# Retention by chunks and a two-layer PReLU block in one program: second batch in parts, last block through all units at once

## The chip, the cores and the metric

The kernel runs on one core of a Trainium2 chip. The metric is the device time of one execution in microseconds (us); lower is better. A profile of one execution shows what each engine did: PE is TensorE's matmuls and PEld its weight loads, DVE is VectorE, ACT is ScalarE, POOL is GpSimd, SP is the engine whose queue issues nearly all DMAs.

## What is computed

For 8 batches and 8 heads, with 576 positions and 64 features a head, retention is a causal product without softmax; its output, heads side by side, is the input of a two-layer block with a PReLU between.

```
scores = scale * q @ k.T                       # per batch and head, 576 x 576
ret    = scores * gamma[h] ** (i - j) for i >= j, else 0
attn   = ret @ v                               # 8 x 8 x 576 x 64, float32
x      = attn.transpose(0, 2, 1, 3).reshape(4608, 512)
h      = x @ w_in                              # 512 -> 2048
g      = max(h, 0) + alpha * min(h, 0)
out    = g @ w_out                             # 2048 -> 512
```

## The kernel before

**Tiles.** The 4608 rows of x are 18 blocks of 256 (`kb`). The 2048 hidden columns are 8 units of 256 (`u`). A cell is one unit of one block: a first product (`unit`, L1079, 24 matmuls of 128 x 256 columns) into the PSUM banks psh, an ACT and DVE chain that makes g (L1087 to L1094), a split of g for the next product (`split_g`, two ACT and two POOL operations, L1103 to L1110), and a second product (`second`, L1128, 12 matmuls of 128 x 512) into the four banks pso, two cells later (LAG). Precision: x, w and g are split into three pieces each, and each product is three matmuls of pieces. The first eight cells (blocks 0 and 1, units 0 to 3) are computed with plain float32 matmuls instead (`unit_plain` L1014, `second_plain` L1045).

**Weights.** There are 32 pieces of weight (4 a unit). They come as 8-byte words and are converted (`convert`: two ACT, three DVE and one POOL operation, L657 to L681), the first 16 in the start and the other 16 during the pass over the blocks, in the tile wa, from where they are stored (`w32`). `split_w` makes three pieces of a weight (ACT L705, POOL L706, DVE L709). SBUF holds the pieces of four units. So the program goes through all blocks with units 0 to 3, keeping partial sums in DRAM (`o_kept`) and x too (`x_kept`), and then through them with units 4 to 7. At the turn, blocks 14 to 17 are visited in a zigzag of two units a visit, in thirteen visits, so that one weight of a new unit can be split while another is in use. Each visit splits x (`split_x`, L980 to L997) and ends with an evacuation of pso (L1146 to L1151).

**Attention.** Positions are in 9 chunks of 64. Batch 0 is computed in three parts of 4, 4 and 1 chunks for all heads at once (`load_part`, `part_transposes` L447, `part_scale` POOL L421, `part_scores` L473, `part_states` L495, `part_carry`, `part_values` L536 and L552, `last_part` L580 to L613), so that the first block of x is there early. Batches 1 to 7 are computed in pairs of heads (32 pairs, numbers 4 to 31 here; `joint`): the ninth chunk's scores (L838, into a psh bank), scores of eight chunks (L846) and their states (L855), both in the two psa banks, chunks of even and odd number in different banks; DVE masks them (L898, L905) and adds the states up (L916 to L927); the values (L787) of a pair are computed in the next pair's joint. The pairs of batch 1, FIRST, use ACT and POOL for some of it (L873, L883, L889, L934) in place of DMA and DVE.

**Order.** Operations are recorded by `do` with an engine, a cost and what they read and write. `plan` then orders them: from due times and the costs in `do` it picks, engine by engine, what runs next, and knows of banks, of the DMA backlog, and of the SBUF port that DVE and POOL share (operations with `lock=True`). Each engine executes its list in that order. Where a room is used again, its next user waits for the last one.

Of the kernel before, what the change touches and what calls it, by code (L numbers as in the profile page):

```python
# [21 lines left out]
def kernel(  # L22
# [316 lines left out]
    LAG, FIRST, APART = 2, range(4, 8), range(5, 8)  # L339
    QUEUE, HOLD_X = (), 100.0  # L340
    GROUPS = (("v0",), ("v1",), ("x",), ("s", "u"))
# [17 lines left out]
    gs = [slot(mlp, f"g{n}", [P, 3, 2, TB]) for n in range(2)]  # L359
    gas = [slot(mlp, f"ga{n}", [P, 2, TB]) for n in range(2)]  # L360
    gts = [slot(mlp, f"gt{n}", [P, 2, TB]) for n in range(2)]
# [16 lines left out]
    room = {(s, i): Gen(wsl[s, i]) for s in range(1, NS) for i in range(4)}  # L378

    def spot(s, i, at, n):  # L380
        return lambda: room[s, i].get().rearrange("p a b -> p (a b)")[:, at * TB:(at + n) * TB]

    def spot_p(x, i):
        return spot(x + 1, i, 0, 4) if x < 2 else spot(3, 0, 2 * i, 2)

    def key_p(x, i, m):
        return (room[x + 1, i], "d", m) if x < 2 else (room[3, 0], "d", i)

    def part(x, i):
        return spot_p(x, i)().rearrange("p (m h d) -> p m h d", h=H, d=D)  # L390

    def sums_of(x, j):
        return spot(x + 1, j // 2, 4 + j % 2, 1)().rearrange("p (c d) -> p c d", d=D)

    def sums_key(x, j):
        return room[x + 1, j // 2], "u", j

    def carry_of(x):
        return spot(1 + x, 1 + x, 4, 1)().rearrange("p (c d) -> p c d", d=D)

    def carry_key(x):
        return room[1 + x, 1 + x], "c"

    def load_part(x, which=(0, 1, 2)):
        j0, j1 = PARTS[x]
        for i in which:
            for m in range((j1 - j0 + 1) // 2):
                s0 = (j0 + 2 * m) * C
                rows = min(P, j1 * C - s0)
                dma(lambda i=i, m=m, rows=rows: part(x, i)[0:rows, m],  # L410
                    lambda i=i, s0=s0, rows=rows: (k, q, v)[i][0, :, s0:s0 + rows].rearrange(
                        "h p d -> p h d"), rows * DM * 4, (), [key_p(x, i, m)],
                    "ACT" if x == 0 and i == 1 else "SP", RATE_256)

    def part_scale(x, i):
        j0, j1 = PARTS[x]
        rows = min(P, (j1 - j0) * C)
        for m in range((j1 - j0 + 1) // 2):
            def f(m=m):
                t = part(x, i)[0:rows, m]  # L420
                nc.gpsimd.tensor_tensor(  # L421
                    out=t, in0=t, in1=tp[0:rows, i - 1, m, :, None].to_broadcast([rows, H, D]),
                    op=ALU.mult)
# [4 lines left out]
    def banks_of(x):  # L428
        while True:
            for b in (psa[0], pso[0], pso[1], pso[2], pso[3]) if x == 0 else (psa[0], psh[1]):  # L430
                yield b

    def part_transposes(x, i, bank):
        t = tT[x, i] = Gen(gs[0]) if x == 0 and i else room[1, 3] if x == 0 else \
            room[2 + i, 3 - 2 * i]

        def at():
            return (t.get().rearrange("p a b c -> p (a b c)") if x == 0 and i else
                    t.get().rearrange("p a b -> p (a b)"))[:, 0:1024].rearrange(
                        "p (c s) -> p c s", c=NPAIR)  # L440
# [16 lines left out]
    def part_scores(x, bank):  # L457
        a = Gen(gs[1]) if x == 0 else room[3, 2]

        def at():  # L460
            return (a.get().rearrange("p a b c -> p (a b c)") if x == 0 else
                    a.get().rearrange("p a b -> p (a b)"))[:, 0:1024].rearrange(
                        "p (h n) -> p h n", h=2)
# [21 lines left out]
    def part_states(x, bank):  # L485
# [16 lines left out]
        for j in range(4):  # L502
            was = sums_key(x, j - 1) if j else carry_key(x) if x else None

            def g(j=j):
                if j == 0 and x == 0:
# [14 lines left out]

    def part_values(x, bank):
        a, at = tat[x]
        qt, qT = tT[x, 1]
        gx = xb[x] = Gen(xs[x])
# [16 lines left out]
        for m in range(2):  # L542
            js = [j for j in (2 * m, 2 * m + 1) if j or x]
# [15 lines left out]
        def xt():  # L559
            return gx.get().rearrange("p c (m q s) -> p q c m s", m=2, q=2)  # L560
        do("ACT", 0.59, lambda: nc.scalar.copy(xt()[:, 0], to(0)), [(pv[0], 0)], [(gx, "p", 0)])
        for h2 in range(2):
            do("ACT", 0.59, lambda h2=h2: nc.scalar.copy(xt()[half(h2), 1], to(1)[half(1 - h2)]),
               [(pv[1], 0)], [(gx, "p", 1 + h2)])

    def last_part():
        t = room[3, 3]

        def tt():
            return spot(3, 3, 0, 2)().rearrange("p (i c s) -> p i c s", i=2, c=NPAIR)  # L570

        def at():
            return spot(3, 3, 2, 2)().rearrange("p (h c s) -> p h c s", h=2, c=NPAIR)
        pt = Gen(psa[0])

        def f():
            to = pt.get().rearrange("p (i c s) -> p i c s", i=2, c=NPAIR)
            for i in range(2):
                for c in range(NPAIR):
                    nc.tensor.transpose(to[:, i, c], part(2, i)[0:C, 0, 2 * c:2 * c + 2].rearrange(  # L580
                        "p h d -> p (h d)"), ident[0:C, 0:C])
        do("PE", 0.8, f, [key_p(2, 0, 0), key_p(2, 1, 0)], [(pt, 0)])
# [19 lines left out]
        def f():  # L602
            to = pv.get()[:, 0:NPAIR * C].rearrange("p (c s) -> p c s", c=NPAIR)
            for c in range(NPAIR):
                for h2 in range(2):
                    nc.tensor.matmul(to[half(h2), c], part(2, 2)[0:C, 0, 2 * c + h2],
                                     at()[0:C, h2, c], start=(c == 0), stop=False,
                                     skip_group_check=True)
            for c in range(NPAIR):
                for h2 in range(2):  # L610
                    for e in range(0, D, 32):
                        o = h2 * D + e
                        nc.tensor.matmul(to[o:o + 32, c], carry_of(2)[half(h2), c, e:e + 32],  # L613
                                         tt()[half(h2), 1, c], start=False, stop=True,
                                         skip_group_check=True)
        do("PE", 0.9, f, [key_p(2, 2, 0), (t, "m", 0), (t, "m", 1), (t, "t"), carry_key(2)], [(pv, 0)])
        gx = xb[2] = Gen(xs[2])
        do("ACT", 0.37, lambda: nc.scalar.copy(
            gx.get()[:, :, 0:C], pv.get()[:, 0:NPAIR * C].rearrange("p (c s) -> p c s", c=NPAIR)),
            [(pv, 0)], [(xb[2], "b", 0)])  # L620
# [74 lines left out]
    def split_w(at, room_=None):  # L695
        u, i = divmod(at, 4)
        if room_:
            g = Gen(room_)
            key = (g, "w", 0)
            dma(lambda: words_of(g)[:, 0:DM], lambda: w32[at], P * DM * 4, [(w32m[at], 0)], [key])  # L700
        else:
            key = plain[at]
        w = w_at[u, i] = Gen(wsl[u % NS, i])
        full = lambda: words_of(key[0])[:, key[2]:key[2] + DM]
        do("ACT", 0.64, lambda: nc.scalar.mul(piece(w.get()[:, 0]), full(), BELOW), [key], [(w, 0)])  # L705
        do("POOL", 1.29, lambda: nc.gpsimd.tensor_tensor(  # L706
            out=piece(w.get()[:, 1]), in0=full(), in1=w.get()[:, 0], op=ALU.subtract),
            [key, (w, 0)], [(w, 1)], lock=True)
        do("DVE", 0.70, lambda: nc.vector.scalar_tensor_tensor(  # L709
            out=piece(w.get()[:, 2]), in0=w.get()[:, 0], scalar=ONE, in1=full(), op0=ALU.mult,  # L710
            op1=ALU.subtract), [key, (w, 0)], [(w, 2)], lock=True)
# [5 lines left out]

    def load_kq(n):
        b, c = pairs[n]
        if n in APART:  # L720
            kx = qx = Gen(wsl[n - 4, 0])
            kx.kx = lambda: words_of(kx)[:, 0:S]
            qx.qx = lambda: words_of(qx)[:, S:2 * S]
        else:
            kx, qx = Gen(kxs), Gen(qxs)
            kx.kx, qx.qx = kx.get, qx.get
        loaded[n] = [kx, qx, None, vnm[n % 2]]
        for x, g, src in (("qx", qx, q), ("kx", kx, k)):
            for a in range(4):
                f0 = (a % 2) * 32  # L730
                dma(lambda t=getattr(g, x), a=a: t().rearrange("p (n r) -> p n r", r=32)[
                        32 * a:32 * a + 32],
                    lambda src=src, a=a, f0=f0: src[b, 2 * c + a // 2].rearrange(
                        "(n t) d -> t n d", t=32)[:, :, f0:f0 + 32], S * P, (), [(g, x, a)],
                    "ACT" if n in QUEUE and x == "qx" else "SP", RATE_128)

    def load_kn(n):
        b, c = pairs[n]
        kn = loaded[n][2] = Gen(kns[n % 2])
        for h2 in range(2):  # L740
            dma(lambda h2=h2: kn.get()[half(1 - h2)],
                lambda h2=h2: k[b, 2 * c + h2].rearrange("(j t) d -> t j d", t=C), S * D * 4, (),
                [(kn, h2)], "ACT" if n in QUEUE else "SP", RATE_256)
# [8 lines left out]
    def operands(n):  # L752
# [3 lines left out]
        def f():  # L756
            qh = qx.qx().rearrange("p (j x r) -> p j x r", x=2, r=32)
            nc.gpsimd.tensor_tensor(out=qh, in0=qh,
                                    in1=tabx[:, None, c, :, None].to_broadcast([P, NJ, 2, 32]),
                                    op=ALU.mult)  # L760
        four = [(qx, "qx", a) for a in range(4)]
        do("POOL", 1.15, f, (), four, lock=True)
        kT, qT = turned[n] = Gen(kTs[n % 2]), Gen(qTs[n % 2])
        for to, x, g in ((kT, "kx", kx), (qT, "qx", qx)):
            do("DVE", 0.77, lambda to=to, fro=getattr(g, x): nc.vector.transpose(to.get(), fro()),
               [(g, x, a) for a in range(4)], [(to, 0)])
# [9 lines left out]
    def values(n, pv):  # L776
# [6 lines left out]
        for i, js in enumerate((range(0, j1), range(j1, NJ))):  # L783
            def f(i=i, js=js):
                for j in js:
                    for h2 in range(2):
                        nc.tensor.matmul(pv[i].get()[half(h2), (j - js[0]) * C:(j - js[0] + 1) * C],  # L787
                                         vns[n % 2][:, h2, j], mt.mt()[:, h2, j], start=True,
                                         stop=True)
            parts.append((0.133 * len(js), f, [(vn, x, h2) for x in "vs" for h2 in range(2)] +  # L790
                          [(mt, x, h2) for h2 in range(2) for x in ("q", 0, 1, "x")],
# [20 lines left out]

    def on_pe(parts, groups):
        for some in groups:
            do("PE", sum(parts[x][0] for x in some), lambda some=some: [parts[x][1]() for x in some],
               [key for x in some for key in parts[x][2]],
               [key for x in some for key in parts[x][3]], kind="half" if not {"v0", "v1"} & set(some) else None)

    def joint(n):
# [11 lines left out]
        ps = [Gen(psa[p2]) for p2 in range(2)]  # L831

        def at(p2):
            return ps[p2].get().rearrange("p (i j s) -> p i j s", i=2, s=C)

        def f():
            for h2 in range(2):
                nc.tensor.matmul(pv[1].get()[half(1 - h2), 7 * C:], kT.get()[half(h2), chunk(NJ - 1)],  # L838
                                 qT.get()[half(h2), chunk(NJ - 1)], start=True, stop=True)
        parts["x"] = 0.03, f, [(kT, 0), (qT, 0)], [(pv[1], "x")]  # L840

        def f():
            for j in range(NJ - 1):
                for h2 in range(2):
                    x = half((1 - h2, h2)[j % 2])
                    nc.tensor.matmul(at(j % 2)[x, 0, j // 2], kT.get()[half(h2), chunk(j)],  # L846
                                     qT.get()[half(h2), chunk(j)], start=True, stop=True,
                                     skip_group_check=True)
        parts["s"] = 0.47, f, [(kT, 0), (qT, 0)], [(ps[0], 0), (ps[1], 0)]

        def f():
            for j in range(NJ - 1):
                for h2 in range(2):
                    x = half((h2, 1 - h2)[j % 2])
                    nc.tensor.matmul(at(j % 2)[x, 1, j // 2], kn.get()[half(1 - h2), j],  # L855
# [483 lines left out]
```

## Time and profile before

| | us |
|---|---|
| median of 3 runs | 961.99 (961.79 to 962.37) |
| the profiled execution | 960.84 |
| its span, first to last instruction | 959.1 |
| from the start to the first split product | 107.3 |

| stretch of the span, us | PE busy | DVE | ACT | POOL |
|---|---|---|---|---|
| 0 to 107.3 | 91.7 | 86.5 | 71.6 | 71.2 |
| 120 to 440 | 318.0 | 236.4 | 203.4 | 213.7 |
| 440 to 545 | 100.1 | 76.5 | 77.4 | 83.6 |

The groups that matter, one row each, with the mean of one operation in ns: L1079 first product 284 (24 to a cell, overlapping), L1128 second product 393 (12 to a cell), L898 masks 483 (96), L916 sums 492 (56), L709 split weight on DVE 964 to 1300, L706 on POOL 1272 to 1498, L669 on the tile wa 924, L705 split weight on ACT 626 to 630.

How to read it: matmuls overlap, so PE's mean duration is not PE's price; the price is the time from the start of one group to the start of the next. A chain piece called "issue" is time in which the engine waited for nothing that the profile shows. DMA share is the mean busy share of the core's 16 DMA engines.

### The profile page before, as it was taken

To read this page: it belongs to the slowest core of one execution; us is meant where nothing else is said; L and a number is where in the kernel's file an instruction comes from. 1 tells how busy PE (TensorE), PEld (TensorE's weight loads), DVE (VectorE), ACT (ScalarE), POOL (GpSimd) and SP (SyncE) were. 2 spreads that over 40 slices of the span, in tenths; PEclk is the share of its full clock that TensorE was granted. 3 is DMA by queue.
4 is the path that set the end of the run, shared out by engine and by line. 5 is a ranking of instruction groups with operands and counts; after the bars stand their busy time and mean duration, and the time that the engine had idled before them with its cause. 6 is when DMAs were issued, how large, how long until landed. Compare 5 with 4: busy or idle time off the path is not lost.

```text
span 959.1 us, 22745 instructions
## 1 busy us (share of the span) xinstructions
PE 927.6 (97%) x8713; PEld 815.9 (85%) x8713; DVE 623.4 (65%) x1292; ACT 592.7 (62%) x1329; POOL 633.0 (66%) x515
## 2 busy tenths in 40 slices
PE   5998799999999999999899999999999999999997
PEld 4766598889888888888788899999999999999996
DVE  6789877777767778777678767564444544444444
ACT  3669756666657576665877666655555555555542
POOL 4759876658758577494887989665555555555543
PEclk9999999999999999999999999999999999999999
DMA  9977687777767778776464644242222112122111
GB/s 235 200 167 149 167 176 189 161 189 187 172 161 175 190 168 182 187 169 177 175 220 143 194 137 132 88 121 78 89 88 67 67 66 67 66 67 66 45 45 66
DMA packets 253341, 131.66 MB, mean 137 GB/s; under 512 B 218144, under 2 KB 218160, under 8 KB 253232
## 3 DMA queue, kind: packets, MB, share of 16 engines
q1 hardware_dynamic: 251120, 129.67, 52.2%
q8 instruction: 68, 1.11, 0.5%
q10 hardware_dynamic: 2112, 0.53, 0.3%
q14 instruction: 41, 0.34, 0.1%
HBM read 81.67 MB, written 35.13 MB: 122 GB/s over the span
## 4 chain that ended last, share of the span: by engine, by line
PE 82%; DVE 3%; ACT 1%; issue 1%; POOLq 0%; POOL 0%; DVEq 0%; ACTq 0%
PE psh L1079 39%; PE pso L1128 37%; PE psh L787 3%; PE psa L846 1%; PE psa L855 1%; DVE wa L667 1%; PE psh L838 1%; DVE ga L1094 0%; DVE o L1151 0%; DVE wa L669 0%; DVE ga L1088 0%; DVE at L898 0%; DVE lx L987 0%; ACT lx L980 0%; ACT psh L1091 0%
## 5 line engine op out<-in xcount | busy, mean ns | idle before, releaser
L1079 PEld LDWEIGHTS psh<-lx,w 128*128 128x128 f32 x3264 | 410.3, 191 | 21.0 <-DVE ga L1094 5.7
L1079 PE MATMUL psh<-lx,w 128*128 128x256 f32 x3264 | 418.8, 284 | 6.1 <-DVE ga L1094 3.3
L1128 PE MATMUL pso<-w,g 128*128 128x512 f32 x1632 | 403.5, 393 | 1.0 <-DVE o L1151 0.7
L1128 PEld LDWEIGHTS pso<-w,g 128*128 128x128 f32 x1632 | 295.8, 189 | 58.0 <-DVE o L1151 1.1
L1107 POOL TENSOR_TENSOR g<-ga,g 128x512 fp32r<-128x512 f32 x136 | 178.0, 1309 | 235.2 <-ACT g L1103 230.5
L1088 DVE SCALAR_TENSOR_TENSOR ga<-psh,gt 128x256 f32<-128x256 f32 x272 | 114.6, 422 | 173.9 <-ACT gt L1087 165.1
L1110 POOL TENSOR_TENSOR g<-g 128x512 fp32r<-128x512 f32 x136 | 177.1, 1302 | 10.8 <-ACT g L1105 0.7
L1094 DVE SCALAR_TENSOR_TENSOR ga<-psh,malpha,ga 128x256 f32<-128x256 f32 x272 | 130.0, 479 | 65.2 <-ACT psh L1091 63.8
L1091 ACT ACTIVATE psh<-ga 128x256 f32<-128x256 f32 x272 | 105.2, 388 | 97.3 <-DVE ga L1088 96.2
L1103 ACT ACTIVATE g<-ga 128x512 fp32r<-128x512 f32 x136 | 86.0, 632 | 117.8 <-PE pso L1128 106.0
L1087 ACT COPY gt<-psh 128x256 f32<-128x256 f32 x272 | 101.1, 372 | 70.8 <-PE psh L1079 62.4
L997 POOL TENSOR_TENSOR lx<-lx 128x512 fp32r<-128x512 f32 x78 | 100.6, 1298 | 17.7 <-DVE lx L987 15.6
L1105 ACT ACTIVATE g<-ga 128x512 fp32r<-128x512 f32 x136 | 84.4, 620 | 0.0
L898 DVE SCALAR_TENSOR_TENSOR at<-psa,pf,mask 64x256 f32<-64x256 f32 x96 | 46.3, 483 | 19.9 <-PE psh L787 10.1
L980 ACT ACTIVATE lx<-x 128x512 fp32r<-128x512 f32 x78 | 48.5, 628 | 0.0
L994 POOL TENSOR_TENSOR lx<-x,lx 128x512 fp32r<-128x512 f32 x30 | 38.8, 1293 | 7.4 <-ACT lx L992 7.3
L1146 DVE TENSOR_TENSOR op<-pso,op 128x512 f32<-128x512 f32 x46 | 31.5, 684 | 14.1 <-PE pso L1128 14.1
L787 PEld LDWEIGHTS psh<-at,vn 128*64 128x64 f32 x900 | 29.0, 138 | 9.6 <-issue 3.6
L987 DVE TENSOR_TENSOR lx<-x,psa 128x512 fp32r<-128x512 f32 x48 | 32.6, 678 | 4.4 <-PE psh L1079 4.3
L787 PE MATMUL psh<-at,vn 128*64 128x64 f32 x900 | 33.6, 226 | 1.5 <-DVE ga L1094 1.5
L806 ACT COPY x<-psh 128x256 f32<-128x256 f32 (+3 forms) x84 | 24.2, 319 | 17.1 <-PE psh L787 11.3
L1151 DVE SCALAR_TENSOR_TENSOR o<-pso,op 128x512 f32<-128x512 f32 x46 | 31.6, 688 | 1.1
(183 smaller groups left out, 864.6 us busy)
## 6 DMA issues: line engine op xcount, KB each, us to landing
ok<-o SPq DMA_DIRECT2D x46, 256.0 KB, 2.9
x<-xk SPq DMA_DIRECT2D x23, 512.0 KB, 4.9
op<-ok SPq DMA_DIRECT2D x23, 512.0 KB, 3.9
xk<-x SPq DMA_DIRECT2D x18, 512.0 KB, 3.7
out_dram<-o SPq DMA_DIRECT2D x36, 256.0 KB, 3.9
kn<-in_k_dram SPq DMA_DIRECT2D x56, 144.0 KB, 3.6
vn<-in_v_dram SPq DMA_DIRECT2D x56, 144.0 KB, 3.4
qx<-in_q_dram SPq DMA_DIRECT2D x100, 72.0 KB, 2.9
```

The lines of the kernel that those rows point to most:

```text
L787: nc.tensor.matmul(pv[i].get()[half(h2), (j - js[0]) * C:(j - js[0] + 1) * C], vns[n % 2][:, h2, j], mt.mt()[:, h2, j], start=True, stop=True)
L997: do("POOL", 1.29, lambda c=c: nc.gpsimd.tensor_tensor(out=piece(to.get()[:, 2, c]), in0=to.get()[:, 0, c], in1=to.get()[:, 1, c], op=ALU. ...
L1079: nc.tensor.matmul(at(b), piece(w[:, l, c0:c0 + P]), piece(x.get()[:, l, cc]), start=(n == 0 and cc == 0), stop=(n > 0 and cc == NCC - 1), ...
L1087: do("ACT", 0.36, lambda t=t, at=at: nc.scalar.copy(t(), at(1)), [(ph, 1)], [(gt, f)])
L1088: do("DVE", 0.42, lambda t=t, g=g, at=at: nc.vector.scalar_tensor_tensor(out=g(), in0=at(0), scalar=ONE, in1=t(), op0=ALU.mult, op1=ALU.su ...
L1091: do("ACT", 0.39, lambda g=g, at=at: nc.scalar.activation(at(1), g(), ACTF.Relu, scale=-1.0), [(ga, f)], [(ph, 1)])
L1094: do("DVE", 0.48, lambda g=g, at=at, fc=fc: nc.vector.scalar_tensor_tensor(out=g(), in0=at(1), scalar=malpha[:, fc:fc + 1], in1=g(), op0=A ...
L1103: do("ACT", 0.64, lambda: nc.scalar.mul(piece(to.get()[:, 2]), ga.get(), BELOW), both, [(to, 2)])
L1105: do("ACT", 0.64, lambda: nc.scalar.mul(piece(to.get()[:, 0]), ga.get(), BELOW * 2.0 ** -12), both, [(to, 0)])
L1107: do("POOL", 1.29, lambda: nc.gpsimd.tensor_tensor(out=piece(to.get()[:, 1]), in0=ga.get(), in1=to.get()[:, 2], op=ALU.subtract), both + [ ...
L1110: do("POOL", 1.29, lambda: nc.gpsimd.tensor_tensor(out=piece(to.get()[:, 2]), in0=to.get()[:, 0], in1=to.get()[:, 1], op=ALU.subtract), [( ...
L1128: nc.tensor.matmul(a[2 * m + b].get(), piece(g.get()[:, l, f, m * P:(m + 1) * P]), piece(w_at[u, 2 + f].get()[:, l]), start=(cell["first"] ...
```

## The change

Batch 1 is computed in parts like batch 0 (part numbers 3, 4, 5, with x // 3 the batch), in the start, among the plain cells; FIRST and its forms are gone, and pair 8 is the first joint. A part's chunks go to whichever block they belong to (`chunk_home`). The zigzag goes: blocks 0 to 16 with units 0 to 3, block 17 with all eight, blocks 0 to 16 with units 4 to 7. The pieces of unit 4 go to rooms that attention no longer needs, those of units 5, 6, 7 to the rooms of units 0, 1, 2; late weights are split with a second ACT operation into PSUM and two DVE operations, without POOL. In a joint, all eight scores have one psa bank and all states the other, and the ninth score's matmuls are recorded with them as one operation. g has three rooms; the room gt is gone, its ACT copy goes into ga. Joints of batches 2 to 7 stand at every second cell (some at every third). Between operations of DVE and POOL that share the SBUF port, and follow each other in the planned order, a dependency is added.

```diff
-    GROUPS = (("v0",), ("v1",), ("x",), ("s", "u"))
+    GROUPS = (("v0",), ("v1",), ("x", "su"))
-    gs = [slot(mlp, f"g{n}", [P, 3, 2, TB]) for n in range(2)]
+    gs = [slot(mlp, f"g{n}", [P, 3, 2, TB]) for n in range(3)]
-    gts = [slot(mlp, f"gt{n}", [P, 2, TB]) for n in range(2)]
...
+    def chunk_home(x, j):
+        kb, o = divmod(x // 3 * NJ + j, TB // C)
+        if kb not in xb:
+            xb[kb] = Gen(xs[kb % NRING])
+        return xb[kb], o
...
-        w = w_at[u, i] = Gen(wsl[u % NS, i])
+        if planes is None:
+            g = Gen(wsl[u if u < NS else u - NS - 1, i])
+            planes = [(g, l) for l in range(3)]
...
+        if raw:
+            hp = Gen(psa[at % 2])
+            do("ACT", 0.6, lambda: nc.scalar.mul(piece(hp.get()), full(), BELOW), [key], [(hp, 0)])
+            do("DVE", 0.69, lambda: nc.vector.tensor_tensor(
+                out=l(), in0=full(), in1=hp.get(), op=ALU.subtract), [key, (hp, 0)], [w[1]])
+            do("DVE", 0.69, lambda: nc.vector.scalar_tensor_tensor(
+                out=d(), in0=hp.get(), scalar=ONE, in1=full(), op0=ALU.mult,
+                op1=ALU.subtract), [key, (hp, 0)], [w[2]])
+            return
...
-                    x = half((1 - h2, h2)[j % 2])
-                    nc.tensor.matmul(at(j % 2)[x, 0, j // 2], kT.get()[half(h2), chunk(j)],
+                    nc.tensor.matmul(chunks(ss)[half(h2), j], kT.get()[half(h2), chunk(j)],
                                      qT.get()[half(h2), chunk(j)], start=True, stop=True,
                                      skip_group_check=True)
...
-                    nc.tensor.matmul(at(j % 2)[x, 1, j // 2], kn.get()[half(1 - h2), j],
+                    nc.tensor.matmul(chunks(uu)[half(h2), j], kn.get()[half(1 - h2), j],
...
-    order += [(kb, (0, 1, 2, 3)) for kb in range(2, 14)]
-    order += [(14, (0, 1)), (15, (0, 1)), (16, (0, 1)), (17, (0, 1, 2, 3)), (16, (2, 3)),
-              (15, (2, 3)), (14, (2, 3, 4, 5)), (15, (4, 5)), (16, (4, 5)), (17, (4, 5, 6, 7)),
-              (16, (6, 7)), (15, (6, 7)), (14, (6, 7))]
-    order += [(kb, (4, 5, 6, 7)) for kb in range(14)]
+    order = [(kb, (0, 1, 2, 3)) for kb in range(NKB - 1)]
+    order += [(NKB - 1, range(NU))]
+    order += [(kb, (4, 5, 6, 7)) for kb in range(NKB - 1)]
...
+    turn = cells.index(next(c for c in cells if c["u"] == NS)) - NS
+    late = {turn - 8 + 2 * i: [16 + i] for i in range(4)}
+    for i in range(3):
+        for n in range(4):
+            late.setdefault(turn + 1 + i + n // 2 * LAG, []).append(20 + 4 * i + n)
...
+    port = None
     for op in best[1]:
         now[0] = best[2][op.n]
-        op.fn()
+        ins = op.fn()
+        if op.lock:
+            if port and port[0] != op.eng:
+                tc.add_manual_dep(ins.ins, port[1].ins.name, mybir.DependencyInfo(
+                    mybir.DependencyClass.Sync, mybir.DependencyReason.DATA), reason="port")
+            port = op.eng, ins
```

## The prediction

> **What bounds the kernel now.** First the page's busy times and slices, for the whole.
>
> ```profile
> span 959.1 us, 22745 instructions
> ...
> PE 927.6 (97%) x8713; PEld 815.9 (85%) x8713; DVE 623.4 (65%) x1292; ACT 592.7 (62%) x1329; POOL 633.0 (66%) x515
> ```
>
> PE is busy 97% of the span, the next engine 66%, so the end is PE's work plus what PE waits. Second, the stretches (time, then busy time of each engine, clock, DMA share, GB/s), for where the waits are.
>
> ```profile
> core 0: us, PE busy (x) PEld busy (x) DVE busy (x) ACT busy (x) POOL busy (x), PEclk, DMA share, GB/s
> 0.00:20.00 20.00, 10.15 (x305) 8.40 (x305) 12.23 (x51) 6.99 (x11) 7.37 (x20) 1.00 0.96 228
> ...
> 80.00:107.30 27.30, 24.95 (x336) 16.86 (x337) 24.77 (x45) 24.59 (x51) 23.30 (x22) 1.00 0.65 135
> 107.30:120.00 12.70, 8.48 (x147) 7.51 (x146) 10.09 (x23) 8.06 (x21) 12.01 (x10) 1.00 0.73 181
> ...
> 440.00:500.00 60.00, 56.17 (x427) 49.34 (x417) 40.21 (x74) 44.56 (x100) 46.12 (x36) 1.00 0.59 193
> ...
> 600.00:945.00 345.00, 345.00 (x2216) 315.06 (x2215) 168.48 (x343) 192.98 (x428) 199.07 (x155) 1.00 0.23 74
> ```
>
> From 600 on PE never pauses; it pauses in the start, at the hand-over from plain to split products (107 to 120), and around the late weights (440 to 545). Third, the chain in a stretch without pauses, for PE's prices (start, us, what).
>
> ```profile
> 228.69 2.75 PE pso L1128 x12
> 231.44 1.20 PE psh L787 x36
> 232.64 0.20 PE psh L838 x2
> ...
> 233.36 0.47 PE psa L855 x32
> 233.83 3.06 PE psh L1079 x24
> ```
>
> A second product is 2.75, a first 2.87 (here 3.06 as the last piece has other shape before it), the values of a pair 1.20, ninth score, scores and states 1.19 together (232.64 to 233.83). Fourth, the chain at the worst pause.
>
> ```profile
> 458.78 1.41 DVE wa L667
> ...
> 460.35 1.17 issue
> 461.52 0.48 DVE ga L1094
> 462.05 1.70 PE psh L1079 x12
> ...
> 472.46 1.22 DVE wa L667
> 473.71 1.42 DVE wa L669
> ```
>
> PE waits for a ga that stands on DVE behind the late conversion of a weight (wa). Fifth, that tile's durations (least/median/most, ns):
>
> ```profile
> L667 DVE TENSOR_SCALAR wa<-wa x16: 416/441/1550, 196.6 to 524.3; 128x512 f32<-128x512 f32 x16
> L669 DVE TENSOR_SCALAR wa<-wa x16: 409/952/1433, 197.4 to 525.5; 128x512 int32<-128x512 int32 x16
> ```
>
> Work of 0.41 us takes up to 1.55 while POOL runs.
>
> **PE's account before.** Starts on PE's timeline, each group's time to the start of the next. After 107.3: 136 cells of 2.87 + 2.75 = 764.3; 24 values and 23 score groups of 1.20 = 56.4; changes of array shape (some 0.1 to 0.2 at each border of a pair's groups) 10.2; from the last product to the end 5.3 beyond the products; the rest of 851.8 is waiting, 15.6: 5.3 at the hand-over, about 7 from 440 to 545, 3.3 between. Before 107.3: about 101.6 of work (with the unavoidable first loads) and 5.7 of waits in the middle (at 79, 91 and 101 us 1.4 to 1.7 each, score groups waiting for DVE, behind a conversion).
>
> **The change, part by part.**
>
> Batch 1 in parts. Removed from PE: four joints, each with 1.09 of scores and states, a lone ninth score 0.26, values in two pieces 0.85 + 0.50: 4 x 2.70 = 10.8. Added: the instructions of a part at part 1's and 2's starts on PE: four transposes 0.44, so 16 take 1.8; scores 1.09; states 1.09; values 3.4 (2.85 in a batch's first part): 6.8 + 7.4, and the ninth chunk 0.70 + 0.61 + 1.19 = 2.5; 16.7. Net +5.9, all on PE's path. Nothing hides it; that is this edit's price. What it takes off the others in the start: ACT 4 x 6.7 (copies L873 0.67, scalings L883 0.47, copies L934 0.62, the rest 2.6) against 9.4 of copies out of PSUM; POOL 4 x 4.9 (L889 0.90 x4, L758 1.15 to 1.47) against ten scalings of 1.04 and two carries of 0.62, 11.6; DVE 4 x 4.3 against 7. So ACT -17, POOL -8, DVE -10 us of some 107, where DVE and ACT were 90% busy from 80 to 107. The batch's loads are 3.5 MB instead of 4.6 (pairs load k twice, 72 KB at a time), 5 to 8 us less of transfer at the 228 to 135 GB/s shown, in a start whose DMA share reaches 0.96 to 0.99. On SP's queue all six 256 KB loads of the batch's first part now stand ahead of weight piece 8, and the rest among pieces 8 to 15, where the pairs' loads stood; no row shows PE waiting for a weight's DMA there, so I take zero, -1 to +3. The 5.7 of waits: mine is 3 left (a part's transposes stand 16 in a row on two banks, each copy 0.59 against 0.44, some 0.7 us; scores behind DVE's conversions). Ends 1 and 8.
>
> Hand-over, 5.3: there POOL was busy 12.0 of 12.7, with split weights (L706, 1.3 to 1.5) and lx, and DVE's qT transposes and split weights stood ahead of the scores. POOL and DVE come 8 to 10 us less loaded, and in the changed order two plain second products (3.6, moved from the start, no cost) stand between the first split product and the next scores. I take 2; ends 0.5 and 5.3.
>
> Scores and states in banks of their own, ninth score joined. PE: 64 small matmuls as before in the same four quadrants; 1.20 stays 1.20. Twelve borders of lone ninth scores go, but values are split more often; the changed order has 23 score groups and 32 of values (35 and 29 before), and its borders at the rows' prices come to 10.4: zero. Joining makes scores wait for the psh bank; their neighbours are values, which wait for it anyway: zero, 0 to +1. DVE: four masks of 0.483 and two sums of 0.492 become two masks (as L479 from PSUM, 0.69) and one sum (as L1088, 0.42): 6.3 a pair becomes 5.2, off PE's path until DVE is late. Of the 3.3 between I leave 2.5, for cells after 120 keep conversions.
>
> Third g room: ACT's split no longer waits for PE's second product two cells back (ACT g on PE pso, 106 us of waits that nothing on PE shows): zero, -1 to 0. The gt room goes, so ACT's copy, not DVE's subtraction, now waits for POOL's reading of ga two cells back. The nearest row is DVE ga L1088 on POOL g L1107, 7.2 us in 5 waits, longest 3.1; behind the copy stand ACT's relu and splits, for which DVE and PE wait. POOL is done a cell ahead except at those 5 places: +0.5 within the joint phase's 2.5, ends 0 and 3.
>
> Last block through eight units. 41 visits become 35: six fewer x loads, split x, twelve fewer evacuations and stores; POOL -15.6 (2.6 each), DVE and ACT less, all hidden now, so no gain by itself. Late weights lose POOL's 1.3 to 1.5 and DVE's 0.96 to 1.30 and take ACT 0.63 + 0.59 (as L984) and DVE 2 x 0.68 (as L987). But twelve pieces crowd into some eight cells (45 us): ACT 12 x 1.22 + 8 x 2.8 + splits 4 = 41, 91%. PE's cell gives the second psh bank 2.75 us for a chain of 1.7 (0.37, 0.42, 0.39, 0.48), so two foreign ACT operations just fit. Of about 7 us I leave 2.5; ends 1 and 7.
>
> Port order: every DVE operation that shares SBUF with POOL now waits for POOL's previous one, and the reverse, 48 late and 16 early operations. Here the Trainium skill speaks against the change ("SBUF — State Buffer", section "Who interferes with whom"): the shared port pair is an exclusive lock, held for the whole instruction, decided by who issues first. By that rule hardware does already what the semaphores do; they can only add a wait for a POOL operation that has not begun, up to one of 1.3, with every later ga of DVE's queue behind it and PE behind that: 16 x 1.3 = +21. The row agrees on the blocking (0.41 becomes 1.55) but shows two blocks in a row, 1.22 then 1.42, POOL slipping in between L667 and L669. In the changed order both stand together behind one POOL wait in 14 of 16, so a conversion saves up to 1.0. I take zero for it inside the 2.5 and 2.5, ends -3 and +21.
>
> **Sum.** 959.1 + 5.9 - 21.3 (all waits) + 3 + 2 + 2.5 + 2.5 = 953.7 span. The profiled execution took 960.84, 1.74 around its span, and the median of the runs is 1.15 above it: 953.7 + 2.9 = 956.6.
>
> **Rivals.** Nearly all waits go, 4 left: 947.7 + 2.9 = 950.6; for it, PE's flawless 600 to 945 and relief on all engines; against, hand-made interleaving in a start that had waits throughout. Chance 0.22. Parts pay nothing: start and hand-over keep their 11, the rest as forecast: 962.6 less the third room's 1, about 961.6; for it, PE is the fuller engine after +5.9; chance 0.10. That is also the case that the edit doesn't relieve what it means to. Slower: the port order. If POOL is behind the planned order when DVE reaches a conversion, DVE stands. It decides from (962.0 - 956.6) / 16 = 0.34 us a conversion that reaches PE; at 0.8 it gives 956.6 + 12.8 = 969. For it, L667 waits in the changed order on POOL; against, POOL has 30% idle there. Chance 0.07. The forecast: 0.61.
>
> The range runs from 948.8 (below the first rival, towards the floor of 943.7 + 2.9) to 962.6 (waits of start and hand-over kept). 0.2%, 1.9 us, is about what a measurement can tell: faster is the forecast, the first rival and a piece of the second, 0.85; same 0.08; slower 0.07.
>
> **What would show it.** First split product near 104 to 107 after the start; DVE wa of 0.4 without pairs above 1.2; no PE pause over 1 us from 440 to 545; 5.62 a cell from 600 on. Wrong if first split products begin after 110, if PE waits for a DVE that waits for POOL, or if ACT's copies hold PE in the last block.

## The result, and the profile after

The changed kernel takes 954.77 us in the median of 7 runs (953.86 to 958.57), the kernel before 961.79 in the same set (7 runs): ratio 0.9937, 95% interval 0.9919 to 0.9955. The forecast was 956.6, range 948.8 to 962.6. The profiled execution is the longest of the seven, 958.57 us with a span of 956.5. A second profile, of the same kernel in experiment 1 (953.37 us, span 951.4), is needed beside it: the two differ only in the start.

The page's first lines, of the first profile:

```profile
span 956.5 us, 22974 instructions
...
PE 930.8 (97%) x9009; PEld 820.8 (86%) x9009; DVE 554.1 (58%) x1180; ACT 573.8 (60%) x1285; POOL 576.8 (60%) x473
```

DVE is 69 us less busy, POOL 56, ACT 19, PE 3 more. The span fell by 2.6 here and by 7.7 in the other profile, so the relief was worth only what PE had waited for it. The stretches, with the columns of before:

```profile
core 0: us, PE busy (x) PEld busy (x) DVE busy (x) ACT busy (x) POOL busy (x), PEclk, DMA share, GB/s
0.00:20.00 20.00, 9.37 (x222) 8.04 (x223) 11.57 (x50) 6.00 (x9) 6.83 (x20) 0.99 0.84 210
80.00:107.30 27.30, 25.61 (x450) 16.95 (x449) 18.08 (x33) 14.34 (x28) 18.29 (x16) 1.00 0.65 144
107.30:120.00 12.70, 12.70 (x121) 9.08 (x120) 8.76 (x19) 6.82 (x17) 10.67 (x9) 1.00 0.41 103
440.00:500.00 60.00, 59.38 (x410) 53.84 (x409) 40.45 (x84) 46.13 (x103) 39.44 (x32) 1.00 0.44 142
600.00:945.00 345.00, 345.00 (x2212) 314.86 (x2211) 165.07 (x336) 191.08 (x426) 194.37 (x152) 1.00 0.21 70
```

In the stretch that held the hand-over before, 107.3 to 120, PE is busy 12.70 of 12.70 us (8.48 before). The hand-over itself now comes at 114.81 in this profile, and from there to 130 the profile shows no wait of PE. With the late weights PE is busy 59.38 of 60 (56.17). From 80 to 107 PE waits less and ACT is down from 24.59 to 14.34. What PE waits for from 440 to 560, first before, then after:

```profile
PE psh L1079 <- DVE ga L1094: 3.3, 4, 1.1
PE psh L1079 <- POOL lx L997: 0.7, 1, 0.7
PE pso L1128 <- DVE o L1151: 0.7, 1, 0.7
```

```profile
PE psh L808 <- DVE ga L1071: 0.6, 1, 0.6
```

(Columns: us in total, times, longest.) The loss is in the start. The chain of the first profile, then of the second, at the same matmul:

```profile
16.91 0.35 PE pso L556 x14
17.26 3.19 issue
20.45 0.58 PE pso L556 x17
```

```profile
16.59 0.35 PE pso L556 x14
16.94 1.30 issue
18.24 0.76 PE pso L556 x46
```

PE stands amid the part's values with no semaphore to wait for, after 14 of 96 matmuls of L556. The kernel before stood at the same count of its instructions, after 14 of L552, for 1.36 us. That count is 222 matmuls and 223 weight loads, as the row 0 to 20 above has it; where the expectations below speak of the 451st record, it is the 446th. In all three traces a 16 KB packet of the instruction queue goes ahead of the end of the pause by 2.3 to 2.5 us: it begins at 15.78 (before), 17.96 and 15.89. After the long pause the clock record shows half clock from 19.57 to 29.82, three stretches of 3.41 us; after the 1.36 of before one of 3.41; in the second profile none until 950. The stretch from 20 to 30, first profile, then second (the third number from the end is the granted clock):

```profile
20.00:30.00 10.00, 8.41 (x98) 6.87 (x98) 6.05 (x10) 4.07 (x7) 4.93 (x5) 0.51 0.95 252
```

```profile
20.00:30.00 10.00, 7.69 (x37) 5.38 (x38) 6.49 (x12) 5.63 (x11) 6.80 (x7) 1.00 1.05 291
```

So there are two kinds of difference, one fixed and one that varies between executions.

**The account.** PE's groups, each to the start of the next, against the prices that the prediction used. "Excess" is what remains: waits and changes of shape. The second profile against the one of before:

| us | forecast | measured |
|---|---|---|
| start, PE's work | +5.9 | +6.1 |
| start, waits | -2.7 | -0.1 (23.2 to 23.0) |
| hand-over, to 120 | -3.3 | -4.9 (5.4 to 0.5) |
| 120 to 440 | -0.8 | -1.0 (12.1 to 11.1, borders in it) |
| 440 to 560 | -4.5 | -7.1 (8.35 to 1.24) |
| after the last product | 0 | -0.7 (5.25 to 4.52) |
| span | -5.4 | -7.7 |

In the first profile everything behind the first split product is the same within 0.1 (17.5 of excess against 17.4), and the start's waits are 28.1.

Two things hide in the start's rows. Two plain second products, 3.6 us, moved from the start to behind the first split product, so the start is only 2.5 longer (109.8 against 107.3). And its waits also hold what half clock costs, of which the second profile has none. PE's idle time before the first split product shows the waits alone: 15.6 us before, 17.6 in the second profile.

### The profile page after: what moved, and what is told of

Same layout as the page of the kernel before. It is cut to its first block, busy times and chain, and to the rows that moved or that the text cites. A ratio compares the mean times of both kernels' runs of the same rounds, so it can differ in the third digit from the quotient of the medians.

```text
span 956.5 us, 22974 instructions
## 1 busy us (share of the span) xinstructions
PE 930.8 (97%) x9009; PEld 820.8 (86%) x9009; DVE 554.1 (58%) x1180; ACT 573.8 (60%) x1285; POOL 576.8 (60%) x473
## 4 chain that ended last, share of the span: by engine, by line
PE 91%; DVE 2%; POOL 2%; ACT 2%; issue 1%; DMA 1%; ACTq 0%; POOLq 0%; DVEq 0%
PE psh L1057 40%; PE pso L1105 39%; PE psh L808 3%; PE pso L1023 2%; PE psh L992 2%; PE psa L870 2%; DMA w<-in_q_dram 1%; PE psh L860 1%; PE psa L867 1%; POOL w L732 1%; ACT x L571 1%; DVE psa L679 0%; POOL w L423 0%; ACT w L669 0%; POOL lx L975 0%
## 5 line engine op out<-in xcount | busy, mean ns | idle before, releaser
L1057 PEld LDWEIGHTS psh<-lx,w 128*128 128x128 f32 x2832 | 356.3, 191 | 11.6 <-DVE ga L1071 0.6
L1057 PE MATMUL psh<-lx,w 128*128 128x256 f32 x2832 | 364.2, 284 | 0.0
L1105 PE MATMUL pso<-w,g 128*128 128x512 f32 x1416 | 350.0, 393 | 1.4 <-DVE o L1128 1.2
L1105 PEld LDWEIGHTS pso<-w,g 128*128 128x128 f32 x1416 | 256.5, 189 | 50.0 <-DVE o L1128 1.4
L1065 DVE SCALAR_TENSOR_TENSOR ga<-psh,ga 128x256 f32<-128x256 f32 x272 | 115.0, 423 | 192.8 <-ACT ga L1064 189.3
L1064 ACT COPY ga<-psh 128x256 f32<-128x256 f32 x272 | 101.3, 373 | 134.7 <-PE psh L1057 118.4
L975 POOL TENSOR_TENSOR lx<-lx 128x512 fp32r<-128x512 f32 x66 | 84.7, 1295 | 44.4 <-DVE lx L965 36.2
L888 DVE SCALAR_TENSOR_TENSOR at<-psa,pf,mask 64x512 f32<-64x512 f32 x48 | 36.0, 750 | 31.6 <-PE psa L867 29.0
L693 POOL TENSOR_TENSOR wa<-wa,op 128x512 int32<-128x512 int32 x16 | 21.0, 1311 | 21.5 <-DVE wa L690 11.7
L1123 DVE TENSOR_TENSOR op<-pso,op 128x512 f32<-128x512 f32 x34 | 23.3, 687 | 15.3 <-PE pso L1105 15.3
```

The source lines that it names most:

```text
L975: do("POOL", 1.29, lambda c=c: nc.gpsimd.tensor_tensor(out=piece(to.get()[:, 2, c]), in0=to.get()[:, 0, c], in1=to.get()[:, 1, c], op=ALU. ...
L1057: nc.tensor.matmul(at(b), w[:, c0:c0 + P], piece(x.get()[:, l, cc]), start=(n == 0 and cc == 0), stop=(n > 0 and cc == NCC - 1), skip_grou ...
L1064: do("ACT", 0.36, lambda g=g, at=at: nc.scalar.copy(g(), at(1)), [(ph, 1)], [(ga, f)])
L1065: do("DVE", 0.42, lambda g=g, at=at: nc.vector.scalar_tensor_tensor(out=g(), in0=at(0), scalar=ONE, in1=g(), op0=ALU.mult, op1=ALU.subtrac ...
L1105: nc.tensor.matmul(a[2 * m + b].get(), piece(g.get()[:, l, f, m * P:(m + 1) * P]), w_piece(u, 2 + f, l), start=(cell["first"] and f == 0 a ...
```

## The experiments

Each was timed in five rounds beside the kernel before, and ratios are to that. Experiments 1 to 4 ran on one chip in one set, 5 to 8 in another, 9 to 11 in a third, 12 in one of its own.

**1. The changed kernel once more** (no edit).

> The changed kernel once more, nothing edited. Its runs so far were 953.9 to 958.6 and its one profile, of the slowest run, shows PE without a wait from 17.26 to 20.45 us in front of its 451st matmul or weight load, and the clock at half from 19.57 to 29.82. Theory: that pause is a fetch of PE's instructions and its length decides how long the clock stays at half; a run with a pause near the 1.36 us of the kernel before shows one half-clock stretch of 3.41 us and a span near 952.5, one with 3.2 us two or three stretches and 954 to 956.5. Rival: clock and pause have nothing to do with each other. Median by both 954 to 955.5.

Measured 954.71 (953.07 to 957.71), ratio 0.9922, 0.9905 to 0.9939. The profile has the pause of 1.30 and no half clock; first split product at 109.80 against 114.81. The short pause goes with a short start, but the one half-clock stretch that the theory had for such a pause is absent. Over the fourteen profiles of this document, pause and clock go together loosely: soon after pauses of 2.62 to 3.19 us come one to three stretches, after 0.35 to 0.93 none, and after those between anything from none (1.30, 1.62, 1.71) to two (0.97, 1.69).

**2. Without the port order.**

```diff
-        if op.lock:
-            if port and port[0] != op.eng:
-                tc.add_manual_dep(...)
-            port = op.eng, ins
```

> The changed kernel without the added dependencies between DVE and POOL; all instructions and their order stay. Theory of the prediction, that these dependencies cost and save next to nothing: within 1 us of the changed kernel, DVE's operations on wa spread up to 1.4 to 1.5 us again. Rival 1, they save the pairs of blocked conversions (up to 1.0 each of 16, where PE waits for DVE): 3 to 8 us slower, pauses of about 1 us on PE in the pass from 120 to 440. Rival 2, DVE stands behind POOL because of them: 2 to 4 us faster.

Measured 956.65 (955.29 to 961.32), ratio 0.9952, 0.9935 to 0.9968: 1.9 slower. The intervals of 1 and 2 touch, but the traces agree on where: the excess from 440 to 560 is 2.73 instead of 1.24, all of it at one place, the chain at 445:

```profile
445.48 1.45 DVE wa L681
446.93 0.02 issue
446.95 1.63 DVE wa L690
448.58 0.41 DVE ga L1071
448.99 0.04 issue
449.03 0.27 PE psh L808
```

The same place in the first profile of the changed kernel:

```profile
448.10 1.31 POOL lx L975
449.42 0.02 issue
449.44 0.44 DVE wa L681
449.88 0.02 issue
449.90 0.69 DVE wa L690
450.59 0.41 DVE ga L1071
451.00 0.04 issue
451.04 0.69 PE psh L808 x16
```

Without the dependencies two conversions (0.44 and 0.69 with them, where the tile's longest L681 is 430 ns) take 1.45 and 1.63 in a row, and PE waits 2.2 us for ga instead of 0.6. One wait in the start is also longer (2.17 against 1.67). So the dependencies save, at one place out of 16, less than rival 1 has it; rival 2 is out, and the prediction's "within 1 us" is missed as well. The trace accounts for 1.5 of the 1.9; by ratio the loss is 2.9.

**3 and 4. Fewer and more bytes of loads under way in the start.** The kernel holds a load back while 1.25 MB are outstanding; here 0.75 and 2 MB.

```diff
-    LIMITED, IN_FLIGHT = 100.0, 5 << 18
+    LIMITED, IN_FLIGHT = 100.0, 3 << 18
```

```diff
-    LIMITED, IN_FLIGHT = 100.0, 5 << 18
+    LIMITED, IN_FLIGHT = 100.0, 8 << 18
```

> The changed kernel with at most 0.75 MB of loads under way in the start instead of 1.25 MB; the order of all instructions stays. Theory, PE's instructions are fetched behind the loads on the same DMA engines: the pause before PE's 451st record falls to 1.4 us or less, the clock is at half for one stretch of 3.41 us at most, and the time falls by 1 to 3 us unless weights come later for it. Rival, the pause is PE's own: 3.2 us again, and the time is 0 to 4 us above the changed kernel since loads start later.

> The changed kernel with at most 2 MB of loads under way in the start instead of 1.25 MB; the order of all instructions stays. Theory, PE's instructions are fetched behind the loads: the pause before PE's 451st record is 3.2 us or more, two or three half-clock stretches, 1 to 3 us slower. Rival, the pause is PE's own: 1.4 to 3.2 us as before, the idle stretch of the loads at 18 to 20 us is gone, and the time falls by 0 to 2 us.

0.75 MB: 955.80 (954.38 to 959.41), ratio 0.9936, 0.9918 to 0.9954. 2 MB: 958.06 (955.86 to 958.40), ratio 0.9952, 0.9937 to 0.9968. The pause is 0.97 and 3.00 us, the packet at 12.67 and 16.83; the instructions and their order are the same in both.

With 2 MB the time went as the theory has it (3.4 slower; the rival had it 0 to 2 faster), and so did the clock (two stretches at 20 us, one at 47), but the pause, 3.00, still lies inside the rival's 1.4 to 3.2. With 0.75 MB the pause is as short as the theory has it. The clock is not: it is at half in three places, at 17, 45 and 96 us, five stretches in all. The time did not fall, as the "unless" had it: a weight's conversion on ACT (L669) waits 2.23 us for its load, the copies of x stand behind it on ACT, and PE waits 2.60 for them in front of the first plain product (1.38 in experiment 1). At 42.49 PE stands a second time without a semaphore, for 1.67 us, amid another part's L556.

One profile each does not settle what makes the pause, since the eight profiles of the changed start with 1.25 MB spread from 0.93 to 3.19; experiments 10 and 12 add two more with few bytes under way, 0.35 and 0.65.

**5, 6 and 7. The late weights: order or way of splitting?** 5 splits them as before (ACT, POOL, DVE), 6 takes the zigzag of before, 7 both.

```diff
-        if raw:
+        if False:
             hp = Gen(psa[at % 2])
```

```diff
-    order = [(kb, (0, 1, 2, 3)) for kb in range(NKB - 1)]
...
+    order += [(14, (0, 1)), (15, (0, 1)), (16, (0, 1)), (17, (0, 1, 2, 3)), (16, (2, 3)),
...
+            split_w(at, Gen((xs[2], xs[3], xs[4], ats)[at % 4]))
```

> The changed kernel, but the late weights (pieces 16 to 31) are split as before: one ACT, one POOL and one DVE operation in place of two ACT and two DVE; the order through the blocks stays. The changed kernel has 1.2 us of excess on PE from 440 to 560, the kernel before 8.35. Theory 1, the split without POOL is what ended the late waits: 3 to 7 us slower than the changed kernel, pauses of 1 us and more from 440 to 545. Theory 2, the order (one block through eight units, each weight needed later and once) ended them: within 1 us of the changed kernel.

> The changed kernel, but blocks 14 to 17 go in the zigzag of before, with the late weights split by ACT and DVE as in the changed kernel. Theory 1 (the split without POOL ended the late waits): within 1 us of the changed kernel. Theory 2 (the order ended them): 3 to 7 us slower, PE waits from 440 to 560.

> The changed kernel, but with the zigzag of before and the late weights split with POOL as before: the late part of the kernel before behind the changed start and joints. By both theories some 7 us slower than the changed kernel, 961 to 962, with 7 to 8 us of excess on PE from 440 to 560; if it is under 958, the late waits of before were owed to something else, the port dependencies or the third g room.

| | eight units | zigzag |
|---|---|---|
| split without POOL: median, ratio, excess 440 to 620 | 954.71, 0.9922, 1.2 | 953.50, 0.9917 (0.9898 to 0.9936), 0.9 |
| split with POOL | 957.22, 0.9949 (0.9932 to 0.9966), 3.5 | 957.71, 0.9959 (0.9942 to 0.9975), 6.0 |

The first entry is experiment 1, from another set of runs. The zigzag edits also put back the rooms and the moments of the late splits.

The way of splitting saves 2.2 us of excess with one order and 5.2 with the other; the order saves 2.6 with POOL and nothing without. Theory 2 falls: with the new split the zigzag is as fast. The times agree: with the zigzag the intervals of the two splits don't meet; with eight units they overlap a little (0.9905 to 0.9939 and 0.9932 to 0.9966), and there the excess carries the reading. The traces show by which way: split with POOL, DVE stands idle for POOL in front of its 16 late operations (L734), 14.4 us in experiment 5 and 18.0 in 7, waits by the port order among them. Split without POOL it stands for POOL in front of none of its 32 (L726, L728), in experiments 1 and 6. In experiment 7 PE's waits of before are back:

```profile
PE psh L1060 <- DVE ga L1074: 2.3, 3, 0.9
PE pso L1108 <- POOL g L1090: 1.1, 1, 1.1
```

Still 7 is 4.8 below the kernel before of its set (962.51; 3.9 by ratio), not level with it, and under the 958 that its expectation set as a mark: part of the late waits of before was owed to something else. That part is 2.3, as the late excess is 6.0 where before has 8.35; which of the other edits took it was not tried. And 7 keeps what those gave elsewhere: 0.4 at the hand-over (5.4 before), 10.6 from 120 to 440 (12.1).

**8. The kernel before with the new order and split of the late weights alone.**

> The kernel before with one part of the change alone: the last block through all eight units, late weights to other rooms and split by ACT and DVE; start, joints, g rooms stay as before and no dependency is added. Theory, the parts of the change add up and the batch in parts costs in the start what it gives at the hand-over: 962 - 7 - 0.7 = 954 to 955, level with the changed kernel; PE's first split product at 107.3 us, 5.3 of excess at the hand-over, 1 to 2 from 440 to 560. Rival 1, the late gain needs relief of the other engines by the rest of the change: 957 to 960. Rival 2, the batch in parts is worth more than this: over 956 with late waits gone.

Edit: the order and `split_w` of the change in the kernel before, as the change's diff has them.

Measured 963.21 (960.83 to 965.82, 22 runs), ratio 1.0002, 0.9992 to 1.0013. No gain: rival 1, and more than it. The hand-over keeps its 5.3, from 120 to 440 the excess is 13.9 (12.1 before), and from 440 to 560 it is 6.9 (8.35). PE's waits there:

```profile
PE psh L1093 <- POOL lx L1011: 2.6, 2, 1.9
PE psh L1093 <- DVE ga L1108: 1.3, 1, 1.3
PE psh L804 <- DVE ga L1108: 1.1, 2, 0.6
```

All lie between 455 and 471 us, where masks of 0.48 and sums of 0.29 of one of the last pairs, a split of x, an evacuation and a conversion stand in a row on DVE. The start of that profile is 3.0 longer, with a second half-clock stretch. So the new late part pays only together with other parts of the change; the rows point to a DVE that still has the heavier pairs to do. Which of the lighter joint, its new places, the third g room and the port order it needs was not separated.

**9. Two rooms for g.**

```diff
-    gs = [slot(mlp, f"g{n}", [P, 3, 2, TB]) for n in range(3)]
+    gs = [slot(mlp, f"g{n}", [P, 3, 2, TB]) for n in range(2)]
```

> The changed kernel with two rooms for g instead of three; the rest as changed, the planner orders anew. Theory of the prediction, ACT's wait for a g room costs PE nothing: within 1 us of the changed kernel (954.7), excess on PE after the first split product 17 to 18.5. Rival, the third room is what hides the conversions and late weights: 2 to 5 us slower, new pauses of PE on ga or g between 120 and 560.

Measured 957.53 (956.20 to 961.82), ratio 0.9962, 0.9949 to 0.9975: 2.8 slower than experiment 1 (3.8 by ratio, and the intervals don't meet). Excess after the first split product is 19.5 against 17.4, 1.8 of it from 120 to 440 and 0.9 after the last product. ACT's waits for a g room from 120 to 560 (experiment 9, then 1):

```profile
ACT g L1080 <- PE pso L1105: 19.4, 20, 1.5
```

```profile
ACT g L1080 <- PE pso L1105: 3.1, 4, 1.5
```

PE's longest entry of the same stretch in experiment 9, which experiment 1 does not have, is for ACT's copies of values:

```profile
PE psh L1057 <- ACT x L827: 1.5, 3, 0.7
```

That fits a hidden wait on ACT that delays what stands behind it. The planner also ordered anew with two rooms, and how much of the 2.8 is the order's was not separated.

**10. Fewer bytes under way for the very first loads only.**

```diff
-                    if eng == "SP" and ahead >= IN_FLIGHT:
+                    if eng == "SP" and ahead >= (3 << 18 if now[0] < 8.0 else IN_FLIGHT):
```

> The changed kernel, but of the very first loads (the part's k, q and v) at most 0.75 MB are under way, and 1.25 MB from the first weight on; order of all instructions unchanged. In the run with 0.75 MB throughout, PE's second wait was 1.25 us instead of 3.04 and the fetch of instructions came at 12.67 instead of 15.9 us, but the weights came late. Theory, loads that nobody needs yet delay the ones that PE starts with: first split product 1 to 3 us earlier than 109.8, median 952 to 954. Rival, the gain is eaten by the wait for the first weights (2.6 us there): within 1 us of the changed kernel.

Measured 952.11 (951.16 to 952.66), ratio 0.9897, 0.9884 to 0.9910. PE's second wait is 1.25 instead of 3.04, the instruction packet comes at 12.82, the pause is 0.35, and the first split product stands at 108.66 although that profile has one half-clock stretch at 43. The four runs lie within 1.5 us; those of the changed kernel spread over 4.7. Operands that come earlier and a shorter pause both follow from this edit, and their shares were not separated.

**11. The ninth score an operation of its own.**

```diff
-    GROUPS = (("v0",), ("v1",), ("x", "su"))
+    GROUPS = (("v0",), ("v1",), ("x",), ("su",))
```

> The changed kernel with the ninth score recorded as an operation of its own, as before, so that the planner may put it apart from the other scores. Theory of the prediction, joining is worth nothing: within 1 us of the changed kernel, the excess of 120 to 440 stays at 11 to 12. Rival, each lone ninth score costs a change of array shape of 0.1 to 0.2: 23 of them, 2 to 4 us slower.

Measured 953.40 (951.88 to 955.70), ratio 0.9913, 0.9898 to 0.9927. Excess after the first split product is 16.0 against 17.4, and the one large pause of 120 to 440 (1.5 at 403 us, where an evacuation on DVE stood behind a joint's masks) is gone. By place the gain is 0.4 at the hand-over, 0.2 from 120 to 440, where something else takes most of that pause back, and 0.8 from 440 to 560. The times alone do not tell 11 from 1 (their intervals overlap), but the five profiles with the changed kernel's order agree within about 0.1 in this excess. So joining costs 1.3 to 1.4.

**12. Both, 10 and 11.**

> The changed kernel with both edits that made it faster alone: the ninth score an operation of its own again (953.40 alone, against 954.71 for the changed kernel in another set of runs), and at most 0.75 MB of the very first loads under way (952.11 alone). Theory, the one ends a wait in the pass and the other a wait in the start, so they add: 950.5 to 951.5, first split product at 108 to 110 us, excess after it 16. Rival, the planner's new order loses in the start what it gains in the pass: 952 to 953.

Measured 949.59 (949.14 to 950.26), ratio 0.9861, 0.9838 to 0.9885. They add, within the intervals, and the time is 0.9 below the lower end of what was expected. First split product 107.74, excess after it 15.9, no half clock until 947. By ratio (0.9861 against 0.9922 to 0.9937) it is 0.6 to 0.8% below the changed kernel.

## Why the prediction was right, and where its steps were not

**Right in the sum, by errors of opposite sign, which is luck in part.** 956.6 was forecast, 954.77 measured. The start's waits came out 2.6 above the forecast, the hand-over 1.6 and the late weights 2.6 below it. PE's floor and prices held: from 600 on PE is busy 345.00 of 345.00, and the new work is 6.1 where 5.9 was forecast.

Of its signs, three came: conversions on wa without pairs of slow ones, no pause over 1 us from 440 to 545, an unbroken PE from 600 on. The first split product did not come between 104 and 107, but at 109.8 and 114.8, the latter past the 110 that it named as a sign of being wrong. Another such sign came in small: at 451 us PE waits 0.6 for a ga that stands on DVE behind POOL (the chain in experiment 2).

**The start's waits** ("mine is 3 left") failed. What was forecast happened where it was forecast: from 60 us to the first split product PE is idle 2.6 us instead of 3.8. But from 24 to 60 us it is idle 4.4 instead of 1.2. Rows of the kernel before, PE's waits from 24 to 107, then of the second profile, from 24 to 62:

```profile
PE psa L846 <- DVE g L678: 2.9, 2, 1.5
PE psh L1014 <- ACT x L563: 0.5, 1, 0.5
```

```profile
PE psh L992 <- POOL lx L693: 1.3, 2, 1.1
PE psh L992 <- DVE ga L1003: 1.3, 1, 1.3
PE pso L1023 <- DVE ga L1003: 1.0, 1, 1.0
```

The two waits of 1.4 and 1.5 for DVE are gone. Now PE waits for a weight's last conversion on POOL, and for a plain cell's ga, which stands on DVE behind the three conversions of a weight (0.70, 0.71, 0.69). That DVE, ACT and POOL are less busy on average does not help where the operation that PE needs stands behind another on its engine. Why conversions and cells meet there in the new order was not tried. So of the second rival, "Parts pay nothing", the half about the start was true.

**Code and clock** were not in the prediction. Its 101.6 of work before the first split product took in the pause of 1.4 at 18 us. That pause's length moves between executions (1.30 and 3.19 in two profiles of one kernel), and the clock moves too. The Trainium skill says ("Runtime: NRT & Kernel Launch", "Instruction fetch mechanics") that instructions come in 16 KB blocks on a DMA queue of the sequencer and that crossing a block is "mostly hidden"; here the block is seen, and hidden it is not. For the clock, "TensorE: Matmul & The Clock Gate", Part 1, has an idle window of about 3.4 us halving it; the half-clock stretches here are multiples of 3.41, but pauses of 0.97 to 1.88, well under such a window, preceded some, and others of 1.30 to 1.71 (experiments 1, 6 and 9) were followed by none there. The two profiles reach the first split product 5.0 us apart (109.80 and 114.81) and differ by 0.1 behind it, so an estimate of what pause and clock are worth is up to 5 us.

**Hand-over**, 5.3 to 2, was mis-sized: 0.5 is left. No run took the batch in parts alone. That its excess stays at 0.0 to 0.5 in experiments 2, 5 to 7, 9 and 11 rules out the port order, the late weights, the third room and the joined score, so parts, joint banks, the joints' places or the lost room gt gave it; which, is not shown. **Late weights**, 7 to 2.5, too: 1.2 in its place. The mechanism, a split without POOL, is shown by 5 to 7 (by way of DVE, which no longer stands behind POOL there: 14.4 us in experiment 5, none in 1). The crowding on ACT that the 2.5 was kept for shows in no wait of PE there. Experiment 8 adds that the split gains nothing in the kernel before, where other waits stand in its place. The prediction put the gain down to the block's order and the split together; in the changed kernel it is the split, and the order adds nothing to it.

**Third room of g**, "zero, -1 to 0", was wrong: 2.8 by experiment 9, 2.1 of it in the excess of its trace. The argument was that nothing of 106 us of ACT's waits shows on PE. That was read from the kernel before, where PE waited for other things; in the changed kernel the room counts. That the next wait shows once the longer ones are gone is the likely reason, not a shown one.

**Joining the ninth score**, "zero, 0 to +1", was too low: it costs 1.3 to 1.4. The sum counted PE's borders and the wait for the psh bank; what it left out is probably that a larger operation leaves the planner fewer places, which no run shows.

**Port order**, zero with ends of -3 and +21, gains 1.9 (experiment 2). Of the two sides the row that showed POOL slipping in between two blocked conversions was right. That semaphores can only add a wait was not the whole: the dependencies keep POOL from coming between two short DVE operations, and one wait for POOL is shorter than two blocked operations (2.2 us of PE's waiting against 0.6). The slower rival, DVE standing for POOL, came in the chain of experiment 2 and cost PE no more than those 0.6.

## What to carry to other kernels

Where one engine is 97% busy, sum its work and its waits apart and place by place: relief of other engines is worth the waits it ends, and a new order makes waits elsewhere. A wait that nothing shows on the bound engine is free only as long as a longer one stands beside it; ask again for each wait in the kernel as it will be. Parts of a change need not add up: the late part alone gave nothing (ratio 1.0002), inside the whole it gave 3.6 us (ratio 0.9959 without it in experiment 7, 0.9922 with it).

## What the runs showed of the hardware

PE stopped at the same place, after 222 matmuls and 223 weight loads, in all fourteen profiles, 0.35 to 3.19 us without a semaphore, and by tendency longer the more bytes of loads were under way: 0.35 to 0.97 in three profiles at 0.75 MB, 0.93 to 3.19 in the ten at 1.25, 3.00 in the one at 2. The instruction queue's packet began 2.3 to 3.0 us before each pause ended. It does not simply follow PE: from PE's 200th matmul or weight load to the packet it took 1.7 us in experiment 1, 3.8 in the first profile, 0.8, 1.0 and 1.6 with 0.75 MB (experiments 10, 12 and 3), 3.2 with 2 MB. Holding back loads that were not yet needed shortened the wait for the first operands too (3.04 to 1.25 us, experiments 1 and 10), although the DMA engines were as busy over the first 20 us (share 0.89 and 0.90).

An operation of DVE that takes 0.43 us alone lasted up to 1.43 while POOL worked beside it (L681 on the tile wa, experiment 2), and 0.43 at most where dependencies kept the two apart (experiment 1).
